# Four late weight loads in unequal pieces: shifting rows between the two halves of the DMA engines

## The chip, the cores and the metric

The kernel runs on one core of one Trainium2 chip. The metric is the device time of one execution in microseconds, the median of several. The core has five engines with queues of their own: TensorE (PE, matrix products; its weight loads are a second row, PEld), VectorE (DVE), ScalarE (ACT), GpSimd (POOL) and SyncE (SP). Data comes from memory through 16 DMA engines. GpSimd issues most of the transfers here (queue q0); instructions, too, are fetched through these engines (q8).

## The reference

Two stages. A sparse attention over 8 batches of 576 positions with 8 heads of 64: half of the heads see a local window of 32, the others every 32nd position. Its output is x, 576 x 512 per batch. Then a spectral mix:

```python
X = np.fft.rfft(x, axis=1)
Xr, Xi = (np.real(X[:, :n_modes]), np.imag(X[:, :n_modes]))          # 64 modes
Yr = np.einsum('bmd,mde->bme', Xr, w_r) - np.einsum('bmd,mde->bme', Xi, w_i)
Yi = np.einsum('bmd,mde->bme', Xr, w_i) + np.einsum('bmd,mde->bme', Xi, w_r)
Y[:, :n_modes] = Yr + 1j * Yi
y = np.fft.irfft(Y, n=S, axis=1)
u = x + y
return (u + np.maximum(u @ w_ch, 0.0)).astype(np.float32)
```

Every mode has its own 512 x 512 matrices w_r and w_i in 4-byte floats, 134 MB for all 64. They are read once, and each is used for only 8 batches.

## The kernel before

The weights are taken in two halves of 256 input rows (all 64 modes of the one half, then all of the other). A tile holds a pair of modes: partitions 0 to 63 hold the real parts, 64 to 127 the imaginary ones. The transfer converts to 2-byte floats on its way.

```python
NWBUF = 5
GUEST = {1: "Y0", 2: "X0", 7: "YT"}      # three early pairs in tiles that are free then

def w_fetch(n=1):
    for _ in range(n):
        i = len(w_tiles)
        if i >= 2 * NM:
            return
        half, m = 1 - i // NM, i % NM
        if i // 2 in GUEST:
            wt = big.tile([128, 2, 4, DM], F16, tag=GUEST[i // 2], name="wt")
        else:
            wt = pw.tile([128, 2, 4, DM], F16, tag="w", name="wt")
        for ri, src in enumerate((moe_w_r, moe_w_i)):
            dst = wt[ds(64 * ri, 64)]
            rows = src[m : m + 2, ds(256 * half, 256), :].rearrange(
                "m (p c) e -> p m (c e)", c=4
            )
            dst = dst.rearrange("p m c e -> p m (c e)")
            ones = range(2)
            if ri and not m:
                ones = [1]
            elif i < 2 * NM - 4:
                nc.gpsimd.dma_start(dst, rows)        # 64 rows x 2 modes x 2048
                continue
            for j in ones:
                nc.gpsimd.dma_start(dst[:, j], rows[:, j])
        w_tiles.extend((wt[:, 0], wt[:, 1]))
```

Pairs are counted from 0 to 63; the last two are loaded one mode at a time. A mode is 16 products of 128x128 weights with 16 columns, and at the end of a pair the next tile is asked for:

```python
def mode(slot, m):
    ...
    for e in range(4):
        for c in range(4):
            nc.tensor.matmul(
                yv[:, mi, e, :], wt[pr, XC[c], ds(128 * e, 128)],
                Xh[half][pr, c, :, :, m], start=(c == 0), stop=(c == 3),
            )
    if m % 2 and (slot or m // 2 not in GUEST):
        w_fetch()
```

The strided heads' inputs are 72 rows for a batch and tensor, loaded as 64 and 8 rows. There are twelve such 8-row transfers, all early, in the order v, q, k for batches 0, 2, 4 and 6:

```python
def load_str(b, nb):
    for vi in (2, 0, 1):
        ...
        if nb == 2:
            nc.gpsimd.dma_start(two[0:64], src[0:64])
        else:
            nc.gpsimd.dma_start(ring[0:64, n, :], src[0:64, b % 2])
        if b % 2 == 0:
            nc.gpsimd.dma_start(two[64:72], src[64:72])
```

The second slot of modes ends so (`again` is n products whose result nobody reads, to keep TensorE going):

```python
for m in range(END, NM):            # modes 54 to 63
    mode(1, m)
    if m < END + 2:
        ...
    else:
        again(0 if m < NM - 6 else 4 if m < NM - 2 else 2)
spec_last(0)
...                                 # inverse transforms, relu, sums, output: all after mode 63
```

The mask `cMl` (128 x 256) is read by the attention over local windows only, which is over when the second slot begins.

Of the kernel before, what the change touches and what calls it, by code (L numbers as in the profile page):

```python
# [79 lines left out]
def kernel(  # L80
# [10 lines left out]
    nc = tc.nc  # L91
# [16 lines left out]
    def psum(kind, half=False):  # L108
# [8 lines left out]
        for n, h in zip(names, hosts)  # L117
# [3 lines left out]
    cs = {  # L121
        n: consts.tile(
            [128, h.shape[1] + more.get(n, 0), *h.shape[2:]], F16, name=n + "_s"
        )
        for n, h in zip(names, hosts)
    }
# [40 lines left out]


    GUEST = {1: "Y0", 2: "X0", 7: "YT"}
    w_tiles = []  # L170
    w_chs = {}
    w_ch = big.tile([128, 4, DM], F16, name="w_ch")

    def w_fetch(n=1):
        for _ in range(n):
# [16 lines that stand above are left out]
                ones = range(2)  # L192
                if ri and not m:
                    ones = [1]
                elif i < 2 * NM - 4:
                    nc.gpsimd.dma_start(dst, rows)  # L196
                    continue
                for j in ones:
                    nc.gpsimd.dma_start(dst[:, j], rows[:, j])
            w_tiles.extend((wt[:, 0], wt[:, 1]))  # L200
# [335 lines left out]
    def mode(slot, m):  # L536
# [8 lines left out]
        for e in range(4):  # L545
            for c in range(4):
# [6 lines left out]
                )  # L553
        if m % 2 and (slot or m // 2 not in GUEST):
            w_fetch()
# [146 lines left out]
    const_load(nc.sync, "cMl", "cFl", "cA")  # L702
    load_str(2, 2)
    w_fetch()

    def str_front(b):
# [39 lines left out]
    for b in range(B):  # L746
        if b in (1, 3):
            load_str(b + 3, 2)
        load_loc(*[(), (), (), (), (0,), (1, 2), (3,), (4, 5)][b])
        w_fetch([2, 1, 1, 1, 1, 1, 0, 0][b])  # L750
        front = str_front(b + 1) if b + 1 < B else loc_front(0)
        for t in range(6):
            str_scores(b, t)
            if b > 0:
                if t < 2:
                    str_values(b - 1, 4 + t)
                elif t == 2:
                    dft(b - 1, 1)
            if t >= 2:
                str_values(b, t - 2)  # L760
            for w in front[SPLIT[t] : SPLIT[t + 1]]:
                w()
        if b == 1:
            nc.vector.memset(PL[:, 0:PS0], 0.0)
# [10 lines left out]
    for b in range(B):  # L775
# [12 lines left out]
        n = 0  # L788
        nm = NMODES[b]
        for mi in range(nm):  # L790
# [3 lines left out]
            n = upto  # L794
# [46 lines left out]
    n = 0  # L841
# [4 lines left out]
    for m in range(END):  # L846
# [7 lines left out]
        n = upto  # L854
# [165 lines left out]
```

The softmax here doesn't subtract the row's maximum and nothing guards it: scores larger than these inputs give would overflow.

## Time and profile before

| what | value |
|---|---|
| time, median of 3 | 434.31 us (433.63 to 435.55) |
| span of the profiled execution | 434.2 us |
| TensorE busy | 338.5 us (78%) |
| VectorE, ScalarE, GpSimd busy | 215.9, 187.5, 129.3 us |
| moved by DMA | 92.18 MB written on the chip's side, 212 GB/s in the mean |
| weight transfers of 512 KB | 62 real, 60 imaginary; 19.0 and 19.4 us from issue to landing |
| weight transfers of 256 KB (one mode) | 4 real, 6 imaginary |

The profile's page cuts the span into 40 equal slices and gives each engine's busy share in tenths; a digit of 9 is 90% or more. Its chain is followed back from the last instruction, at each step to what released it. A line of a group or of the timeline reads: line, engine, operation, output<-inputs, sizes, count, and what ended the idle time before it. "DMA share" is the mean busy share of the 16 DMA engines; it can come out slightly above 1, since packets of one engine overlap a little.

### The profile page before, as it was taken

The numbers are of one execution on the slowest core, as the hardware profiler recorded it, in microseconds if no ns is written. First come the engines' busy times: TensorE is split into PE (matmuls) and PEld (weight loads), VectorE is DVE, ScalarE is ACT, GpSimd is POOL, SyncE is SP. The second block draws the span as 40 slices with busy tenths as digits, with TensorE's granted clock in tenths as the row PEclk, the third lists the DMA queues.
The fourth block names the chain that finished last, engine by engine and source line by source line (L and its number), as shares of the span: only waits on it lengthen the run. The fifth ranks groups of instructions, "written<-read, shape, count | busy, mean of one in ns | idle before, by whom it ended". The sixth has DMA issues, their size and how long they took to land.

```text
span 434.2 us, 12103 instructions
## 1 busy us (share of the span) xinstructions
PE 338.5 (78%) x5307; PEld 244.5 (56%) x5307; DVE 215.9 (50%) x468; ACT 187.5 (43%) x352; POOL 129.3 (30%) x208
## 2 busy tenths in 40 slices
PE   1986888779985787889885566587789798968993
PEld 1865776658864575667753344454456465643441
DVE  2888678744433243342511033355436366503894
ACT  1686678634643435444440401143215123602892
POOL 6433332322332222222222222222222221200992
PEclk9999899865985859875865569887958899988999
DMA  8999999999999999999999999999999999991787
GB/s 176 210 211 213 214 212 213 211 211 213 213 212 212 214 214 212 214 214 213 214 212 213 213 214 214 212 214 215 211 214 214 212 214 214 213 182 30 272 330 261
DMA packets 29140, 92.18 MB, mean 212 GB/s; under 512 B 4064, under 2 KB 5344, under 8 KB 29088
## 3 DMA queue, kind: packets, MB, share of 16 engines
q0 software_dynamic: 24704, 81.28, 94.4%
q1 hardware_dynamic: 3584, 9.59, 5.9%
q8 instruction: 42, 0.69, 0.6%
q10 hardware_dynamic: 800, 0.54, 0.5%
q14 instruction: 10, 0.08, 0.0%
HBM read 163.22 MB, written 9.44 MB: 398 GB/s over the span
## 4 chain that ended last, share of the span: by engine, by line
DMA 68%; PE 19%; DVE 6%; ACT 2%; issue 2%; POOL 1%; DVEq 0%; POOLq 0%
DMA wt<-in_moe_w_i_dram 51%; DMA wt<-in_moe_w_r_dram 11%; DMA ring<-in_q_dram 5%; PE y L547 2%; PE v L689 2%; DVE xb L250 2%; DVE kz L292 2%; PE u L689 2%; PE v L895 2%; PE sc L514 1%; ACT X L260 1%; PE tp L395 1%; DVE rec L249 1%; PE sc L441 1%; PE sc L353 1%
## 5 line engine op out<-in xcount | busy, mean ns | idle before, releaser
L547 PE MATMUL y<-X,wt 128*128 128x16 f16 (+1 forms) x2048 | 82.4, 192 | 61.0 <-DMA wt<-in_moe_w_i_dram 59.4
L547 PEld LDWEIGHTS <-wt 128*128 128x128 f16 (+1 forms) x2048 | 72.9, 103 | 76.5 <-issue 68.5
L196 POOL DMA_DIRECT2D wt<-in_moe_w_r_dram x62 | 36.5, 589 | 141.7 <-PE y L547 67.4
L196 POOL DMA_DIRECT2D wt<-in_moe_w_i_dram x60 | 35.4, 590 | 73.5 <-DMA wt<-in_moe_w_i_dram 61.2
L654 ACT ACTIVATE v<-sc 128x512 f16<-128x512 f32 x32 | 19.1, 597 | 69.7 <-PE sc L645 69.6
L645 PE MATMUL sc<-w_cp,xT 128*128 128x512 f16 (+1 forms) x160 | 48.2, 430 | 0.0
L471 ACT ACTIVATE PL<-sc 128x480 f16<-128x480 f32 (+1 forms) x48 | 27.3, 580 | 46.8 <-PE sc L457 46.5
L655 DVE COPY xo<-tp 128x512 f16<-128x512 f16 x32 | 22.1, 692 | 35.7 <-PE tp L653 35.6
L249 DVE RECIPROCAL rec<-av 90x4 f32<-90x4 f32 (+2 forms) x80 | 14.7, 184 | 46.2 <-PE av L486 34.8
L250 DVE TENSOR_TENSOR xb<-av,rec 90x256 f16<-90x256 f32 (+2 forms) x80 | 36.0, 450 | 2.7
L402 DVE COPY qT<-tp 128x576 f16<-128x576 f16 x16 | 12.0, 758 | 38.8 <-PE tp L395 35.9
L260 ACT ACTIVATE v<-tp 128x640 f16<-128x640 f16 (+1 forms) x24 | 19.4, 808 | 24.9 <-PE tp L429 22.1
L395 PE MATMUL tp<-cI_s,ring 64*64 64x64 f16 x864 | 26.7, 213 | 0.8 <-DVE qT L402 0.6
L360 ACT ACTIVATE PL<-sc 90x360 f16<-90x360 f32 (+1 forms) x48 | 22.7, 491 | 6.1 <-PE sc L353 5.3
L929 DVE TENSOR_TENSOR osb<-u,rl 128x512 f32<-128x512 f32 (+1 forms) x37 | 23.7, 674 | 1.8 <-PE u L689 1.1
L395 PEld LDWEIGHTS <-ring 64*64 64x64 f16 x864 | 21.1, 125 | 5.7 <-issue 2.6
L910 POOL TENSOR_TENSOR rl<-rl,xo 128x512 f32<-128x512 f32 x16 | 18.3, 1157 | 18.2 <-ACT rl L908 17.9
L441 PE MATMUL sc<-cMl_s,cI_s 128*128 128x480 f16 (+1 forms) x48 | 22.5, 468 | 1.6 <-ACT X L260 1.6
L457 PE MATMUL sc<-qT,kz 128*128 128x160 f16 (+1 forms) x160 | 22.4, 267 | 0.0
L908 ACT ACTIVATE rl<-v 128x512 f32<-128x512 f32 x36 | 20.4, 600 | 4.7 <-PE v L689 3.9
L285 PE MATMUL tp<-cI_s,ring 72*128 72x72 f16 x256 | 15.1, 206 | 9.4 <-DMA ring<-in_v_dram 7.9
L260 ACT ACTIVATE kz<-tp 64x360 f16<-64x360 f16 (+1 forms) x32 | 19.1, 595 | 7.7 <-PE tp L395 6.1
(103 smaller groups left out, 655.7 us busy)
## 6 DMA issues: line engine op xcount, KB each, us to landing
wt<-in_moe_w_r_dram POOLq DMA_DIRECT2D x62, 512.0 KB, 19.0
wt<-in_moe_w_i_dram POOLq DMA_DIRECT2D x60, 512.0 KB, 19.4
out_dram<-osb SPq DMA_DIRECT2D x14, 512.0 KB, 2.7
ring<-in_v_dram POOLq DMA_DIRECT2D x8, 288.0 KB, 13.3
ring<-in_q_dram POOLq DMA_DIRECT2D x8, 288.0 KB, 13.6
ring<-in_k_dram POOLq DMA_DIRECT2D x8, 288.0 KB, 13.5
ring<-in_v_dram POOLq DMA_DIRECT2D x3, 512.0 KB, 15.0
ring<-in_q_dram POOLq DMA_DIRECT2D x3, 512.0 KB, 14.8
```

The lines of the kernel that those rows point to most:

```text
L196: nc.gpsimd.dma_start(dst, rows)
L250: nc.vector.tensor_tensor(out=dst, in0=val.rearrange("p h (q c) -> p h c q", c=4), in1=rec[0:n, 0:pieces] .to_broadcast((n, pieces, 64)) . ...
L260: nc.scalar.activation(out=out, in_=in_, func=ACTF.Copy)
L360: nc.scalar.activation(out=PS[0:n, ds(POFF[t], 4 * n)], in_=scp[0:n, 0 : 4 * n], func=ACTF.Exp, scale=SCALE,)
L395: nc.tensor.transpose(tp[ds(64 * hp, 64), ds(64 * i, 64)], qn[ds(64 * hp, 64), ds(64 * (9 * g + i), 64)], idn[ds(64 * hp, 64), ds(64 * hp, ...
L441: nc.tensor.matmul(scp[:, 0 : n * times].rearrange("p (h x) -> p h x", h=times), idn, mask_rows("cMl", n, times), start=True, stop=False,)
L457: nc.tensor.matmul(scp[:, ds(col, n)], kzs[par][:, hp, ds(s0, 128)], qTs[par][:, ds(s0, n)], start=False, stop=(i == len(todo) - 1),)
L471: nc.scalar.activation(out=dst, in_=src, func=ACTF.Exp, scale=SCALE)
L547: nc.tensor.matmul(yv[:, mi, e, :], wt[pr, XC[c], ds(128 * e, 128)], Xh[half][pr, c, :, :, m], start=(c == 0), stop=(c == 3),)
L645: nc.tensor.matmul(vp[pr, :], xT[:, ch, cols], w_chs["cp"][:, ch, :], start=(ch == 0), stop=(ch == 3),)
L655: nc.vector.tensor_copy(out=xo[pr].rearrange("p (h q c) -> p h q c", h=2, c=4), in_=tp[pr, 0:512].rearrange("p (h c q) -> p h q c", h=2, c=4),
L929: nc.vector.tensor_tensor(out=osb[:, t % 2, cols], in0=up[:, cols], in1=rls[b, t][:, t % 2, cols], op=AluOp.add,)
```

## The change

The real part of four late pairs (36, 41, 46 and 51) is loaded as 48, 8 and 8 rows in place of 64. Between the two 8-row pieces stands an 8-row transfer of next to nothing (8 rows of 2 x 8 elements of `w_ch` into the mask tile, which is free by then); its data is never read. A second one follows the real part of the next pair. Each of the eight writes to a place of its own, so none waits for another's write. They are there to turn the choice of DMA engines: an 8-row transfer occupies eight of the 16, and the next one the others, so with a turn in between both 8-row pieces go to the same eight. The purpose is to give those eight more of the weights and the other eight less. The bytes of the weights stay the same, and so does all arithmetic.

```diff
+    UNEVEN = (36, 41, 46, 51)
...
+    turns = []
+
+    def turn_engines():
+        n = len(turns)
+        turns.append(n)
+        dst = cs["cMl"][0:8, ds(32 * n, 32)].rearrange("p (a x) -> p a x", a=2)
+        src = moe_w_ch[0:8].rearrange("p (a x) -> p a x", a=2)
+        nc.gpsimd.dma_start(dst[:, :, 0:8], src[:, :, 0:8])
...
                 if ri and not m:
                     ones = [1]
+                elif i // 2 in UNEVEN and not ri:
+                    nc.gpsimd.dma_start(dst[0:48], rows[0:48])
+                    nc.gpsimd.dma_start(dst[48:56], rows[48:56])
+                    turn_engines()
+                    nc.gpsimd.dma_start(dst[56:64], rows[56:64])
+                    continue
                 elif i < 2 * NM - 4:
                     nc.gpsimd.dma_start(dst, rows)
+                    if not ri and i // 2 - 1 in UNEVEN:
+                        turn_engines()
                     continue
```

## The prediction

> **What bounds the kernel now.** I read four views, from the whole to the end. First the page's 40 slices, its DMA queues and its chain:
>
> ```profile
> PE   1986888779985787889885566587789798968993
> DMA  8999999999999999999999999999999999991787
> q0 software_dynamic: 24704, 81.28, 94.4%
> q8 instruction: 42, 0.69, 0.6%
> q14 instruction: 10, 0.08, 0.0%
> DMA 68%; PE 19%; DVE 6%; ACT 2%; issue 2%; POOL 1%; DVEq 0%; POOLq 0%
> ```
>
> The DMA row stands at 9 from the second slice to the 36th: the weights' queue (q0) keeps all 16 engines full up to some 390 us, and then a tail of 41 us follows in which they no longer matter. 68% of the chain is DMA. Then the waits of TensorE in the second half, and the busy time in stretches around the last weights:
>
> ```profile
> PE y L547 <- DMA wt<-in_moe_w_i_dram: 41.0, 23, 4.2
> ```
>
> ```profile
> core 0: us, PE busy (x) PEld busy (x) DVE busy (x) ACT busy (x) POOL busy (x), PEclk, DMA share, GB/s
> 378.00:387.50 9.50, 6.01 (x91) 3.83 (x92) 0.71 (x2) 0.18 (x1) 1.55 (x3) 0.84 1.05 210
> 388.00:392.00 4.00, 2.94 (x42) 1.61 (x40) 0.56 (x1) 0.00 (x0) 0.00 (x0) 1.00 0.54 108
> 392.00:393.00 1.00, 0.12 (x5) 0.15 (x5) 0.00 (x0) 0.00 (x0) 0.00 (x0) 1.00 0.31 61
> 393.00:394.00 1.00, 0.96 (x18) 0.46 (x16) 0.00 (x0) 0.00 (x0) 0.00 (x0) 1.00 0.02 4
> ```
>
> This is the view that the change is about. From 388 to 392 the share of DMA is 0.54: half of the engines are done some 5 us before the other half, and every transfer is finished only when its slowest engine is. The end itself, on TensorE (start, duration, what it waited for):
>
> ```profile
> 384.17 0.64 PE L547 MATMUL y<-X,wt 128*128 128x16 f16 x16 [3.26 <-DMA wt<-in_moe_w_i_dram]
> ...
> 392.88 0.64 PE L547 MATMUL y<-X,wt 128*128 128x16 f16 x16 [1.95 <-DMA wt<-in_moe_w_i_dram]
> ...
> 394.08 0.64 PE L547 MATMUL y<-X,wt 128*128 128x16 f16 x16
> ```
>
> Modes 62 and 63 start at 392.88 and 394.08 because their weights land then; what follows hangs on mode 63. So the time moves one to one with the last landing.
>
> **Which engines are late, and why.** The packet records behind the DMA row have no engine numbers, but they can be linked: in the full stretch a 4 KB packet takes 324 ns, the next on its engine starts 305 ns after it, and a 64-row transfer gives each engine 8 packets and a completion write, 2457.6 ns in all, over and over. An instruction fetch (q8: 16 KB, 892 to 975 ns) breaks exactly one such rhythm and sets it back by 0.9 to 1.16 us, some 1.1 in most. The fetches take turns over 8 engines: their durations repeat with a period of 8, and an engine hit by one fetch is hit again 8 fetches later. 40 fetches fall before the last weight, five on each of the eight: about 5 us, which is the gap above. The last packets of the eight end at 392.4, 392.6 (four of them), 393.1, 393.2 and 393.6 us.
>
> **What the skill says.** "DMA: Bandwidth & Descriptors", section "Why a DMA increments its semaphore by 16 and not by 1": a transfer uses the largest number of engines up to 16 that divides its slowest dimension; from the software queue, fewer than 16 are consecutive engines from a round-robin cursor. The trace agrees: in the 8-row loads of the strided heads eight engines move two packets each and eight move none, and the next 8-row load takes the other eight. The same section says that only the full count of all 16 means landed, which is the 0.54 stretch seen from the waiting side. Its section "Issuing engines are not separate DMA queues" says that all queues run on the same 16 engines; the fetches of q8 delaying q0 show it. I find no page that says which engines fetch instructions.
>
> **The change, part by part.**
> 1. Real part of an uneven pair: 48 rows are 3 rows, 6 packets, on each engine. The first 8-row piece puts 2 packets on eight engines, the turning transfer moves the cursor on by eight, the second piece meets the same eight again. So a half H has 10 packets and the other half L has 6, where all had 8. The second turning transfer, before the imaginary part of the next pair, puts the cursor back, so all four pairs load the same H. Sum: 4 x 2 x 0.305 us = 2.44 us more on H, 2.44 us less on L.
> 2. Extra transfers: 3 in each uneven pair and 1 in the next, 16 in all. In the 8-row loads an engine with data pays one more completion write (20 ns), one without pays some 15 ns over the usual (its writes follow at 3, 19 and 6 ns). Four pairs: 4 x (2 x 20 + 2 x 15) = 0.3 us on H; about as much on L, as the turning transfers' tiny packets run there. An estimate from these rows: +0.3 us on both.
> 3. GpSimd's issues: 16 more by 0.57 us (the 8-row loads' median) = 9 us spread over 100 us of the engine's idle time; not on the path.
> 4. Buffers and depth: a transfer issues only when the one eight before it has landed (eight completion semaphores in turn). Landing takes 19.4 us, eight times 2.46, so the line is full now. Around an uneven pair the eight places hold small pieces: at least 22 packets, 6.7 us, stay queued on the slowest engine. It doesn't run dry.
> 5. TensorE, VectorE and ScalarE: the same instructions; only landing times shift.
>
> So everything hangs on whether H keeps clear of the eight fetching engines. If L were exactly these, they would end 2.44 - 0.3 = 2.1 us earlier (393.6 -> 391.5), the others at about 391, and the time would be 434.3 - 2.1 = 432.2 us.
>
> **Is it so? What the trace says.** I followed the 16 rhythms through the loads of batches 4 and 6 (the 7th to 12th 8-row transfer). The pieces that the change adds are transfers 13, 15, 17, ...: odd in that count, the half that carried the first (v) 8-row piece of batch 4. Call it H. The third and fourth fetch of the steady part (the two of 893 ns) hit engines of H: one whose completion was due at 57.12 us (raw time) vanished from its place and came 877 ns later, and it is hit again by the fetch eight places on. The next six (949, 945, 935, 974, 974, 961 ns) hit engines of L. So the fetching eight are 6 in L and 2 in H; the halves that the cursor makes stand two engines off. Then:
> - six fetching engines in L end about 2.1 us earlier, the last at 391.5;
> - two fetching engines in H end later. Followed to the end they are among the early ones of the eight, at 392.4 and 392.6; with 2.44 + 0.3 they end at 395.2 and 395.3 us;
> - six others in H, done near 387.5 to 388, end near 390.5.
> The last landing moves from 393.6 to about 395.3, by +1.7 us; mode 62 from 392.88 to 394.6, mode 63 from 394.08 to 395.8. Time: 434.3 + 1.7 = 436.0 us.
>
> **Rivals.**
> - *The halves fit in the changed run* (432.2 us). The size of the change speaks for it: four pairs shift 4.9 us between the halves, the very gap, as if made for halves that fit. If the cursor's place at the start is left over from what ran before, it can differ from this trace. Against it: the one trace I have says 6 and 2, and both kernels move the cursor by whole turns (12 x 8 = 96, and 16 more x 8), so neither shifts it for the next.
> - *The line runs shallow*: with eight places full of small pieces the engines could starve. 6.7 us are left on the slowest; engines of L that don't fetch may idle, but they are up to 10 us ahead and end nothing. Worth 0, or +0.5 us if issue latency bites.
> - *It is hidden anyway*: if the tail were held by ScalarE or VectorE, 434.3 would stay. Against it stand the wait of 1.95 us before mode 62 and the full TensorE after mode 63.
> - *Completion overhead is larger than thought*, because small packets cost more than their bytes: 16 transfers at 0.1 us would add 1.6 us to either case.
>
> **Range and chances.** I give the halves as in the trace 70%, fitting halves 25%, no effect 5%. Two peaks, 432.2 and 436.0, each with some 0.6 us of spread between runs (433.63 to 435.55 before): 432.0 to 437.2 holds a little over eight in ten. I name 435.8, a little under the upper peak. All of this is below 1%: faster by over 2% 0.01, within 2% 0.975, slower by over 2% 0.015.
>
> **What would show it.** In the changed kernel's stretches after 388 us, a half-filled DMA (0.5) that is gone, with the last weights landing near 391.5, shows the fitting halves. A step that thins out early and a thin rest (two engines of 16, a share near 0.13) up to 395 shows the 6 and 2. Mode 63 at about 392 or about 395.8 decides. The 8-row pieces must give two packets to eight engines and both pieces to the same ones; if the heavy half changes from pair to pair, step 1 is wrong and the time stays. A wait of GpSimd on small pieces with DMA below 9 in slices 22 to 32 would show the shallow line. The prediction is wrong if the time falls below 432 or if the last landing moves and the end doesn't.

## The result and the profile after

| kernel | median | lowest to highest | runs |
|---|---|---|---|
| before | 434.53 us | 433.63 to 435.85 | 6 |
| changed | 438.0 us | 436.74 to 439.75 | 6 |

The ratio is 1.0077, with a 95% interval of 1.0056 to 1.0099: the change makes the kernel 3.5 us slower. The prediction was 435.8 us, with 437.2 as its upper end. The time is some 2 us longer than the profiled span in all these runs.

The page of the changed kernel, the rows that were shown for the kernel before, and the GB/s row:

```profile
DMA  8999999999999999999999999999999999990787
GB/s 172 204 210 213 214 212 213 212 210 212 213 213 213 213 213 214 213 214 213 215 212 213 214 204 213 212 211 213 210 213 191 206 212 215 212 210 18 276 330 262
DMA 74%; PE 14%; DVE 5%; issue 3%; ACT 2%; POOL 1%; DVEq 0%; POOLq 0%
```

The DMA row still stands at 9 through the weights, and DMA's share of the chain went from 68% to 74%. But slices 24 and 31 moved 204 and 191 GB/s where their neighbours moved 213: the engines were busy there, and slower. Next the busy time in stretches (length; busy time of the five engines; TensorE's clock; DMA share; GB/s):

```profile
core 0: us, PE busy (x) PEld busy (x) DVE busy (x) ACT busy (x) POOL busy (x), PEclk, DMA share, GB/s
388.00:392.00 4.00, 4.00 (x52) 2.05 (x49) 0.00 (x0) 0.00 (x0) 0.35 (x1) 0.61 1.07 215
392.00:393.00 1.00, 1.00 (x7) 0.43 (x6) 0.00 (x0) 0.00 (x0) 0.00 (x0) 0.84 0.54 102
393.00:394.00 1.00, 1.00 (x20) 0.69 (x19) 0.34 (x1) 0.00 (x0) 0.00 (x0) 1.00 0.33 66
394.00:396.00 2.00, 0.42 (x2) 0.00 (x0) 0.22 (x1) 0.00 (x0) 0.00 (x0) 1.00 0.12 25
```

The half-filled stretch from 388 to 392 (0.54 before) is full now, and at the end a share of 0.12 is left, which is two engines of 16. TensorE's timeline at the end:

```profile
396.25 0.64 PE L565 MATMUL y<-X,wt 128*128 128x16 f16 x16 [1.83 <-DMA wt<-in_moe_w_i_dram]
...
397.51 0.64 PE L565 MATMUL y<-X,wt 128*128 128x16 f16 x16 [0.18 <-DMA wt<-in_moe_w_i_dram]
```

Modes 62 and 63 start at 396.25 and 397.51 us, 3.4 us later than before; the last weights land at 397.0 instead of 393.6. The span grew by 1.8 us only (436.0 against 434.2), because the part from mode 63 on took 38.5 us here and 40.1 in the profiled run of before, with TensorE's clock in the six microseconds after mode 63 at 1.00 and 0.72. The change is not the reason: of the sixteen runs below, ten have 38.0 to 38.8 us there at a clock of 1.00, and three have 40.2 to 40.4 at 0.72 or 0.73. So a single execution can be some 2 us longer or shorter for this alone, and I go by the landings in a trace and by the medians of the times.

There is one more thing to take off. Count the 4 KB packets of the weights' queue in the order of their starts, and ask how much later the same number starts than in the trace of before; I call it the **lag**. It shows how far the engines together are behind. It is 0.5 us at 70 us already, where the two kernels do the same, and still 0.5 ahead of the first uneven pair. So of the 3.4 us between the two landings 2.9 can be the change's; the medians differ by 3.5 us (2.4 to 4.3).

**Where the other half came from.** Compare the stretch around the last uneven pair. Before:

```profile
core 0: us, PE busy (x) PEld busy (x) DVE busy (x) ACT busy (x) POOL busy (x), PEclk, DMA share, GB/s
330.00:335.00 5.00, 4.97 (x77) 3.44 (x75) 3.38 (x8) 4.32 (x8) 1.84 (x4) 1.00 1.06 212
335.00:340.00 5.00, 3.34 (x71) 2.68 (x69) 3.42 (x7) 2.17 (x4) 1.48 (x3) 1.00 1.06 215
```

and changed:

```profile
330.00:335.00 5.00, 4.80 (x66) 3.06 (x65) 3.22 (x8) 3.02 (x6) 0.58 (x1) 0.91 1.06 184
335.00:340.00 5.00, 3.81 (x62) 2.57 (x59) 2.93 (x8) 3.23 (x6) 2.92 (x5) 1.00 1.01 181
```

The DMA share hardly moves (1.06, 1.01), but GB/s falls to 184 and 181: 10 us x (213 - 182.5) / 213 = 1.4 us lost on the mean engine. The packet records say how: 114 packets of 4 KB took 345 to 1006 ns instead of 324, together 18.5 us of engine time too long, and 3.3 us more of idle engines; (18.5 + 3.3) / 16 = 1.4 us again. In the trace of before no 10 us between 60 us and the last weights lose more than 0.6 us of engine time in this way. I call it a slow stretch. The lag says the same: 0.5 us ahead of pair 36, 1.4 at 325 us and 3.0 at 350. The last uneven pair costs the mean engine 1.6 us, the three before it 0.9 together. How much of it fell on the two engines of the thin rest is an estimate: linked back from the last two landings, 1.65 and 1.1 us between 334 and 346 us, but inside a slow stretch more than one link fits.

TensorE's modes are a poorer measure. Against the kernel before they are 1.5 us late at mode 100 and 3.9 at mode 104, a step of 2.4 us; but the ninth run below, which has no uneven pair at that place, steps from -0.3 to 1.3 between the same two modes.

What GpSimd, which issues the loads, did there (start, duration, idle time before and what ended it):

```profile
318.81 0.56 POOL L182 DMA_DIRECT2D cMl_s<-in_moe_w_ch_dram  x1 [1.90 <-DMA wt<-in_moe_w_r_dram]
321.27 0.55 POOL L209 DMA_DIRECT2D wt<-in_moe_w_r_dram  x1 [1.90 <-DMA wt<-in_moe_w_i_dram]
...
329.42 0.57 POOL L182 DMA_DIRECT2D cMl_s<-in_moe_w_ch_dram  x1 [2.38 <-DMA wt<-in_moe_w_r_dram]
333.04 0.58 POOL L212 DMA_DIRECT2D wt<-in_moe_w_i_dram  x1 [3.06 <-DMA wt<-in_moe_w_i_dram]
```

Each small piece waits for the landing of a whole earlier transfer, 2.46 us at the steady pace, as if it were 512 KB itself. While it holds its place among the eight, that much less data is queued. So the theory that the experiments test has two terms: **misfit** (two fetching engines stand in the heavy half, +1.7 us, as predicted) and **the short line** (small pieces use up places, the engines that are ahead run short, and a slow stretch follows that hits the late engines too). The prediction had allowed 0 to 0.5 us for the second.

### The profile page after: what moved, and what is told of

Its sections match the earlier page's. It is cut to its first block, busy times and chain, and to the rows that moved or that the text cites. A ratio compares the mean times of both kernels' runs of the same rounds, so it can differ in the third digit from the quotient of the medians.

```text
span 436.0 us, 12125 instructions
## 1 busy us (share of the span) xinstructions
PE 335.1 (77%) x5307; PEld 241.8 (55%) x5307; DVE 215.6 (49%) x468; ACT 187.4 (43%) x352; POOL 137.5 (32%) x224
## 4 chain that ended last, share of the span: by engine, by line
DMA 74%; PE 14%; DVE 5%; issue 3%; ACT 2%; POOL 1%; DVEq 0%; POOLq 0%
DMA wt<-in_moe_w_i_dram 45%; DMA wt<-in_moe_w_r_dram 19%; DMA ring<-in_k_dram 6%; DMA ring<-in_q_dram 3%; PE v L707 2%; PE u L707 2%; PE v L913 2%; PE sc L532 1%; DVE kz L310 1%; DVE xb L268 1%; DMA ring<-in_v_dram 1%; PE y L565 1%; ACT X L278 1%; POOL wt L212 1%; PE av L392 1%
## 5 line engine op out<-in xcount | busy, mean ns | idle before, releaser
L212 POOL DMA_DIRECT2D wt<-in_moe_w_r_dram x58 | 34.0, 586 | 113.4 <-PE y L565 45.2
L672 ACT ACTIVATE v<-sc 128x512 f16<-128x512 f32 x32 | 19.1, 597 | 73.3 <-PE sc L663 73.2
L663 PE MATMUL sc<-w_cp,xT 128*128 128x512 f16 (+1 forms) x160 | 49.5, 439 | 0.0
```

Of the source, the lines that this page charges most:

```text
L663: nc.tensor.matmul(vp[pr, :], xT[:, ch, cols], w_chs["cp"][:, ch, :], start=(ch == 0), stop=(ch == 3),)
```

## The experiments

Times are medians; each ratio is against runs of the kernel before on the same chip. "Lost" is engine time per 10 us in packets over 324 ns.

**1 to 3. Shift the halves.** If another start of the cursor makes the light half fit the fetching engines, the change pays. A tiny transfer of r rows moves the cursor by r; it is put back after pair 52.

```diff
+                    if i // 2 == 36:
+                        move_cursor(2)          # second run: (8, 4, 2); third: (8)
...
+                        if i // 2 == 52:
+                            move_cursor(8, 4, 2)  # second run: (2); third: (8)
```

> One 2-row transfer before the first uneven pair moves the cursor by 2 (8, 4 and 2 rows after the last one bring it back). Misfit theory: the heavy half then meets either none or four of the eight fetching engines. None: no half-filled and no thin stretch before the last weights, which land near 391.5; time 432.2 us if the pieces themselves cost nothing, 434 us if they cost 1.7 us in any case (line theory). Four: a thin rest of four engines (DMA share near 0.25) before the end, time 437 to 438.5 us. Line theory alone (the halves do not matter): 438 us, as in the changed kernel.

> The same with 14 before (8, 4 and 2 rows) and 2 after. Misfit theory: the other of the two outcomes of the +2 run, that is four heavy fetching engines and 437 to 438.5 us if +2 met none, and 432.2 to 434 us if +2 met four. Line theory alone: 438 us.

> One 8-row transfer before and one after: the other half is the heavy one, and six fetching engines are in it. Misfit theory: a thin rest of six engines (share near 0.37) before the last weights; the last landing was 393.6 and moves by 2.44 + 0.3, time 437.2 us, or 438.9 us with 1.7 us for the pieces. Line theory alone: 438 us.

Measured: +2 gives 438.14 us (ratio 1.0074, 1.0052 to 1.0096), -2 gives 440.45 (1.0116, 1.0082 to 1.0149), +8 gives 439.85 (1.0106, 1.0067 to 1.0145), all against 435.09. None fits. The +2 run looks like the four heavy engines of the misfit theory (a DMA share of 0.27 from 394 to 396 us); then -2 should have fitted, and it took longer than any time expected for it. The +8 run, too, is above all that was expected. With +8 the roles are exchanged: the rest is thick, eight to six engines from 395 to 396 us, where it was two:

```profile
core 0: us, PE busy (x) PEld busy (x) DVE busy (x) ACT busy (x) POOL busy (x), PEclk, DMA share, GB/s
393.00:394.00 1.00, 1.00 (x14) 0.62 (x13) 0.00 (x0) 0.00 (x0) 0.00 (x0) 0.95 1.06 209
394.00:396.00 2.00, 1.21 (x16) 0.48 (x12) 0.56 (x1) 0.00 (x0) 0.00 (x0) 1.00 0.62 123
```

That is the misfit seen from the other side, though not alone: the +8 run also lost 22.5 us in slow packets at 300 to 320 us. The -2 run is spoilt as a test of fit: its three extra transfers in a row at pair 36 left 4 active engines of 16 at one moment near 256 us and 33 us of idle engine time, and the +2 run has 28 us of it at 330 to 340 us: the first signs that the line itself matters.

**4. The same pieces, balanced.** The turn stands behind both 8-row pieces, so they go to opposite halves: all small transfers remain, but no half gets more.

```diff
                     nc.gpsimd.dma_start(dst[48:56], rows[48:56])
-                    turn_engines()
                     nc.gpsimd.dma_start(dst[56:64], rows[56:64])
+                    turn_engines()
```

> The turning transfer stands after the two 8-row pieces, so they go to different halves and each engine has 8 packets as before; the same number and sizes of transfers. Misfit theory: the half-filled stretch of 5 us stays, the last weights land where they did, time 434.5 to 434.9 us. Line theory (the small pieces cost 1.7 us or more by themselves): 436.2 us or more.

Measured: 436.05 us against 435.09, ratio 1.0022 (1.0010 to 1.0034). That is +1.0 us (0.4 to 1.5), between the two expectations, which were 0.4 us at most and 1.7 us at least. So the pieces by themselves cost about 1 us, and most of the 3.5 us comes from the unevenness or through it. In stretches:

```profile
core 0: us, PE busy (x) PEld busy (x) DVE busy (x) ACT busy (x) POOL busy (x), PEclk, DMA share, GB/s
392.00:393.00 1.00, 0.00 (x0) 0.00 (x0) 0.00 (x0) 0.00 (x0) 0.00 (x0) 1.00 0.52 102
393.00:394.00 1.00, 0.57 (x17) 0.60 (x18) 0.00 (x0) 0.00 (x0) 0.00 (x0) 1.00 0.31 61
394.00:396.00 2.00, 1.78 (x25) 0.75 (x22) 0.29 (x1) 0.00 (x0) 0.00 (x0) 0.99 0.00 0
```

The half-filled end is back (0.52) and there is no thin rest: the last weights land at 394.2 us. Lost at 330 to 340 us: 2.4 us, not 18.5. (Near the first of the four pairs, at 255 to 265 us, it lost 6 us.)

**5 to 7. Shifts spread over earlier pairs, and uneven pairs further apart.** The shift by 14 again, its small transfers now at pairs 20, 24 and 28 (fifth run) or 8, 9 and 10 (sixth); the sixth and seventh have their uneven pairs at 13, 25, 39 and 53, the seventh without a shift.

```diff
+    MOVES = {20: 8, 24: 4, 28: 2, 54: 2}    # sixth run: {8: 8, 9: 4, 10: 2, 58: 2}
...
-    UNEVEN = (36, 41, 46, 51)
+    UNEVEN = (13, 25, 39, 53)               # sixth and seventh run
```

> The cursor is moved by 14 as in the -2 run, but by three tiny transfers far apart (after the real parts of pairs 20, 24 and 28) and back by 2 after pair 54, so that the first uneven pair meets a full line; the rest as in the changed kernel. If the -2 run lost its time only because its three moving transfers emptied the line at pair 36, and its halves do fit: no half-filled and no thin stretch at the end, last weights near 391.5 to 392.5, time 2 us below before, 433 us. If small pieces in late pairs cost time whatever the halves: 437 to 440 us, as in the three shifted runs so far.

> Fitting halves (14 moved after pairs 8, 9 and 10), and the four uneven pairs spread over the run (13, 25, 39, 53), one after each round of eight fetches, so that no engine gets more than some 2 us ahead. Theory of the runaway engines (engines far ahead run dry while small pieces hold the eight places, and come back together with long packets): no burst of long packets anywhere, time 2 us below before, 433 us, the last weights at 391.5. If the pieces cost time by themselves: 435 us or more.

> The changed kernel's halves (two fetching engines in the heavy half) with the uneven pairs at 13, 25, 39 and 53. Misfit alone: a thin rest of two engines (share 0.13), mode 63 later by 1.7 us, time 436.6 us. If the remaining 1.3 us of the changed kernel come from engines running ahead they stay away here unless the last pair meets a lead of over 7 us; if the lead does it again at pair 53: 438 us.

Measured: 438.36 (ratio 1.0082, 1.0057 to 1.0107), 437.47 (1.0059, 1.0037 to 1.0081) and 438.10 us (1.0084, 1.0055 to 1.0112), all against 434.81. My halves were wrong again: two engines stay in a thin rest in all three, to 395.7, 396.9 and 397.4 us. And setting the pairs apart did not remove the slow stretches (13.0 us lost at 340 to 350 us in the seventh run).

**8 and 11. Drain the line alone.** The kernel before with seven, then four, tiny 16-row transfers ahead of pair 36. Each gives every engine a packet or two of 16 bytes, so nothing becomes uneven; only places are taken.

```diff
+                    if i // 2 == 36 and not ri:
+                        for _ in range(7):      # eleventh run: 4
+                            move_cursor(16)
```

> The kernel before, with seven 16-row transfers of next to nothing ahead of pair 36: no engine gets more than another, but seven of the eight places hold nothing. Theory of the empty line: the number of active engines falls well below 16 near 256 us, packets of 0.5 to 1 us follow, and the time rises by 1.5 to 2.5 us, to some 437 us, with all engines late alike and the 5 us stretch of eight engines at the end shorter or gone. If a drained line costs nothing because the queue is refilled in time: 435 us.

> The kernel before with four tiny 16-row transfers ahead of pair 36, where the run with seven of them took 5.2 us more. Theory: about four of the eight places in the line can be spared, so the engines hardly run dry: +0.3 to +1.0 us, 435.1 to 435.8, and few packets over 345 ns near 256 us. Rival, each place taken costs the same: four sevenths of 5.2 us, +3.0 us, 437.8.

Measured: seven give 440.0 us against 434.81 (1.0112, 1.0085 to 1.0140), +5.2 us and more than expected; four give 435.29 against 435.06 (1.0007, 0.9994 to 1.0020), within the measurement. GpSimd with seven, and the stretches:

```profile
251.33 0.50 POOL L182 DMA_DIRECT2D scrap<-in_moe_w_ch_dram  x1 [1.94 <-DMA wt<-in_moe_w_i_dram]
253.75 0.50 POOL L182 DMA_DIRECT2D scrap<-in_moe_w_ch_dram  x1 [1.92 <-DMA wt<-in_moe_w_r_dram]
256.54 0.58 POOL L209 DMA_DIRECT2D wt<-in_moe_w_r_dram  x1 [2.30 <-DMA wt<-in_moe_w_i_dram]
257.12 0.60 POOL L209 DMA_DIRECT2D wt<-in_moe_w_i_dram  x1
```

```profile
core 0: us, PE busy (x) PEld busy (x) DVE busy (x) ACT busy (x) POOL busy (x), PEclk, DMA share, GB/s
252.00:256.00 4.00, 2.05 (x31) 1.46 (x28) 2.31 (x6) 0.00 (x0) 0.50 (x1) 0.50 0.42 74
256.00:260.00 4.00, 3.70 (x46) 2.41 (x46) 1.04 (x2) 0.60 (x1) 3.46 (x7) 0.50 0.59 84
```

From the third on, every tiny transfer waited for one full landing (1.9 to 2.0 us), while nothing replaced what landed; then all was empty (shares 0.42 and 0.59, 77 us of idle engine time) and eight loads went out one behind the other without a wait. With four, the same place keeps its share:

```profile
252.00:256.00 4.00, 1.98 (x39) 1.57 (x39) 1.85 (x6) 0.00 (x0) 1.12 (x2) 0.50 1.11 201
256.00:260.00 4.00, 3.08 (x30) 1.86 (x28) 1.85 (x4) 0.60 (x1) 2.96 (x6) 0.50 1.02 190
```

It does have a slow stretch (201 and 190 GB/s, 13.8 us lost) and yet costs nothing measurable: the lag grows by 1.0 us there and stays, but the last weights land only 0.2 us later than before. So a slow stretch is not always time. I read this as engines that end early having lost what they could spare; which engines lost it was not followed.

**9 and 10. Take the change apart.** Three uneven pairs without the last; then the last alone.

```diff
-    UNEVEN = (36, 41, 46, 51)
+    UNEVEN = (36, 41, 46)                   # tenth run: (51,)
```

> The changed kernel with three uneven pairs (36, 41, 46) in place of four. Theory A, the emptied line: with less lead for the eight light engines they do not run dry at the last uneven pair, so there is no stretch of lengthened packets near 330 us and no jump of 2.4 us in the modes' lateness there; modes 100 to 120 about 1.5 us late as before it, last landing about +1.5 to +1.9 us over the kernel before, time about 436.0 to 436.5. Rival B, every uneven pair costs the same share: three quarters of the changed kernel's 3.5 us, time 437.2, modes late in equal steps. Theory C, misfit alone: two heavy engines fetch instructions and carry 3 x 0.61 us more plus overhead, +1.3 us, 435.9.

> Only the last of the four uneven pairs (51), everything else as before. Theory A, the line empties at the fourth uneven pair because the light engines are far ahead by then: alone it is as harmless as the first was, modes up to 0.8 us late after it, last landing at most +0.8 us, time 434.9 to 435.6. Rival, the place itself is costly (pair 51 meets the fetches of the last bands): the step of 2.4 us stays, time about 437.2.

Measured: three give 436.32 (1.0032, 1.0018 to 1.0046), the last alone 435.39 (1.0009, 0.9997 to 1.0022), both against 435.06. That is +1.3 and +0.3, and 1.6 us is not 3.5: by the times, **the parts don't add up**. In the trace with three pairs no slow stretch stands out (at most 3.4 us lost in any 10 us), and the thin rest is there and ends sooner:

```profile
core 0: us, PE busy (x) PEld busy (x) DVE busy (x) ACT busy (x) POOL busy (x), PEclk, DMA share, GB/s
392.00:393.00 1.00, 0.43 (x3) 0.00 (x0) 0.23 (x1) 0.00 (x0) 0.00 (x0) 1.00 0.12 25
393.00:394.00 1.00, 0.41 (x14) 0.44 (x15) 0.00 (x0) 0.00 (x0) 0.00 (x0) 1.00 0.14 29
```

So this trace shows the misfit nearly by itself. Its last weights land at 394.4 us, 0.7 later than before, and its lag ahead of pair 36 is -0.1, so 0.8 us are added. The prediction's terms give 392.6 + 3 x 0.61 + 0.2 = 394.6 us, +1.0 and not three quarters of 1.7, because the two heavy engines first use up the 1.0 us by which they were ahead of the last one. But the profiled execution was the fastest of the twenty (435.13 us; the median is 436.32), so the other executions may well have slow stretches. The tenth run is a half miss: I expected no slow stretch with one uneven pair, and it has one of the largest (27 us of engine time lost at 320 to 340 us, down to 178 GB/s):

```profile
325.00:330.00 5.00, 3.70 (x30) 2.27 (x31) 0.99 (x2) 0.59 (x1) 0.99 (x2) 0.72 1.12 178
330.00:335.00 5.00, 4.97 (x74) 3.39 (x73) 3.69 (x9) 3.34 (x6) 1.75 (x4) 0.94 1.02 187
```

By the median of the times it costs 0.3 us. This trace doesn't show it as free: the last weights land at 395.31 us, 1.7 later than before, of which 0.6 was there before pair 51 (the lag) and 1.0 came after it. The part after mode 63 was short here, 38.0 us against 40.1. Taken by landings, three pairs add 0.8 us, the last alone 1.0 and all four together 2.9: the parts don't add up here either, but 1.0 us is missing and not 1.9.

**12. Mark the cursor.** The kernel before with a 2-row tiny transfer at every second pair from 44 to 58.

```diff
+                    if 44 <= i // 2 < 60 and i % 4 == 0 and not ri:
+                        move_cursor(2)
```

> The kernel before with a two-row tiny transfer after the real part of every second pair from 44 to 58, eight in all, which together take the cursor round once and mark two engines each as early or late. If six or eight engines fetch instructions in the order worked out from the earlier runs (0 or 1, 6 or 7, 9 to 14), the marks in the order 0-1, 2-3, ... 14-15 show late engines in the first, the fourth (or third), the fifth and then two late ones in the sixth and seventh and one in the eighth. Time: single places taken with whole transfers between them, so no emptied line: +0 to +0.6 us; but from one mark to the next the real parts start 2 engines on, and with 64 rows they stay even, so no shift: 434.8 to 435.4. A rival that each tiny transfer costs 0.5 us would give 438.8.

Measured: 435.55 against 435.06 (1.0012, 0.9998 to 1.0026). The two packets of each mark ran at (us):

```
291.79 293.11 | 302.42 303.45 | 311.48 315.74 | 321.62 325.61 | 331.03 336.16 | 345.86 345.92 | 355.81 357.14 | 361.18 366.89
```

Four marks have an early and a late engine (4 to 5.7 us apart), the first two only early ones and the sixth and seventh only late ones (they continue the row of the late packets, some 10 us from mark to mark). That is 4 + 4 = 8 late engines in this trace, but not in the order that I had written down: counted from the first mark, one each of 4-5, 6-7, 8-9 and 14-15, and all of 10 to 13. A window of eight from 0 holds two of them, the complement six, as in the changed kernel; and no window of eight neighbours avoids all, since one late engine stands at 14 or 15 and another at 4 or 5. That fits the shifts, none of which helped.

**13 to 16. The missing term.** The parts left 1.9 us by the times, 1.0 by the landings. First, a shortened line at pair 51 without a fourth uneven pair: the ninth kernel with four tiny transfers ahead of pair 51.

```diff
-    UNEVEN = (36, 41, 46, 51)
+    UNEVEN = (36, 41, 46)
...
+                    if i // 2 == 51 and not ri:
+                        for _ in range(4):
+                            move_cursor(16)
```

> Three uneven pairs (36, 41, 46) and four tiny 16-row transfers ahead of pair 51, which take places in the line without making a pair uneven. Theory: the line empties at pair 51, the early engines come back in step, and the packets of the two engines that are already last lengthen by 1 to 1.7 us: 436.3 + 1.1 to 1.7 = 437.4 to 438.0. Rival, the emptied line costs nothing (as four such transfers ahead of pair 36 did in the kernel before, +0.2): 436.3 to 436.6.

Measured: 437.83 us against 434.63 (1.0072, 1.0046 to 1.0097), inside the theory's range and outside the rival's. Four tiny transfers cost 0.2 us in the kernel before and some 1.7 us here (1.0072 less 1.0032, of 434.6; with the two intervals some 0.5 to 3 us), where two engines are already last. Its trace has two slow stretches:

```profile
305.00:310.00 5.00, 4.21 (x52) 2.64 (x50) 1.94 (x5) 1.19 (x2) 1.36 (x3) 0.86 1.08 190
330.00:335.00 5.00, 3.44 (x52) 2.57 (x51) 2.63 (x6) 2.95 (x5) 2.17 (x4) 0.87 1.03 200
```

The second is the one that was meant; the lag grows by 1.1 us over it, from 2.4 to 3.5. The first stands at pair 46, ahead of the added transfers, where the program is still that of the ninth run, whose trace has 208 GB/s there. So the same program has a slow stretch in one execution and none in another. That a slow stretch is dearer where two engines are already last fits these runs but is not shown: the two drains stand at different pairs (36 and 51), and four tiny transfers ahead of pair 51 in the kernel before were not run.

Then the other half, four uneven pairs without the slow stretch. I moved them forward.

```diff
-    UNEVEN = (36, 41, 46, 51)
+    UNEVEN = (31, 36, 41, 46)               # last run: (10, 14, 18, 22)
...
+    scrap = big.tile([128, 32 * 16], F16, name="scrap")   # not in the first of the three
-        dst = cs["cMl"][0:8, ds(32 * n, 32)].rearrange("p (a x) -> p a x", a=2)
+        dst = scrap[0:8, ds(32 * n, 32)].rearrange("p (a x) -> p a x", a=2)
```

> Four uneven pairs at 31, 36, 41 and 46, none at 51. Theory, misfit and the lengthened packets at pair 51 are two terms: only the misfit is left, which the prediction put at 1.7 us, so 436.5 to 437.0 us, the modes' lateness without the jump of 2.4 us at 330 us, two engines in the thin rest to about 395.3. Rival, the fourth uneven pair costs most wherever it stands: 438 us as the changed kernel.

> Four uneven pairs at 31, 36, 41 and 46, none at 51, the turning transfers written to a place that nothing else uses. Theory, misfit and the lengthened packets at pair 51 are two terms: only the misfit is left, which the prediction put at 1.7 us, so 436.3 to 437.0 us, the modes' lateness without the jump of 2.4 us at 330 us, two engines in the thin rest to about 395.3. Rival, the fourth uneven pair costs most wherever it stands: 438 us as the changed kernel.

> Four uneven pairs at 10, 14, 18 and 22, the turning transfers written to a place of their own. Theory, the line empties only where the fast engines are far ahead, and the misfit is a term of its own: no lengthened stretch (under 3 us of engine time in any 10 us), two engines in the thin rest at the end, +1.7 us over the kernel before (1.2 to 2.2). Rival, an uneven pair empties the line wherever it stands: lengthened stretches in the early part too, and +3 us or more.

The first of the three took 448.93 us and says nothing on the question: at pair 31 the turning transfers go into the mask that the attention over local windows still reads (they change it), and GpSimd then stood 13.27 us waiting for TensorE's modes. With a place of their own: 437.62 against 435.92 (1.0045, 1.0028 to 1.0062), +1.7 us in number as expected (the time itself is above the range, because the kernel before took 435.92 us on that chip), but the trace has a slow stretch at pair 46 (19.1 us lost at 300 to 310 us), so it isn't the misfit alone. The last was to settle that and turned out against me: 438.73 against 434.71 (1.0094, 1.0064 to 1.0124), +4.0 us, with 20.7 us lost at 160 to 200 us. A place early in the program does not protect. The four-pair misfit was never had without a slow stretch; with three pairs it was, in one trace.

## Why the prediction was wrong, step by step

- **Which engines are late: right.** The 16-byte packets of the changed kernel's first turn, which run on the light half, came at 251.61 and 252.44 us, then six from 254.99 to 256.79: two early engines and six late ones, so two late ones are in the heavy half. The thin rest of 0.12 is these two.
- **Step 1, 2.44 us: right; step 2, 0.3 us: too small for all that the pieces do.** In the ninth run a heavy engine can be followed through pair 46: six packets, then two and two, end at 302.07, 302.70 and 303.34 us, started at 300.22; 3.12 us where the usual is 2.46. That is 0.66 us for 0.61 plus overhead, and the second turn adds 0.03. But with the pieces balanced, where step 2 is all that is left, the fourth run took 1.0 us more (0.4 to 1.5).
- **Step 3, GpSimd's issues off the path: right.** They took 0.56 us each (0.57 predicted). What I did not count is that each waits for a landing.
- **Step 4, "It doesn't run dry", and the rival's "Worth 0, or +0.5 us if issue latency bites": this failed.** The 22 packets were worked out for the slowest engine alone, and I took that for enough. Engines ran short (some 13 of 16 active at the least near 334 us), and packets lengthened: the mean engine lost 1.6 us at the last uneven pair. What the prediction's +1.7 us leaves unexplained, and what this term of 0 to 0.5 us has to hold, is 1.2 us by the landings (2.9 less 1.7) and 1.8 us by the times (3.5 less 1.7). The fourteenth run, which shortens the line after three uneven pairs, gives some 1.7 us, with the wide interval and the doubts named there.
- **Step 5, the last landing: right in its logic, wrong in its size.** It was to move by +1.7 us and is 3.4 us later in the trace, 393.6 to 397.0, with 0.5 of it from before the kernels differ. Mode 63 followed it (397.51 instead of 395.8). The median time did, too (438.0 instead of 436.0), but a single execution need not: the part after mode 63 alone varies by 2 us.
- **The sign that I had named for the short line was blind.** "DMA below 9 in slices 22 to 32": the digits stay at 9, because a packet that takes 1000 ns is as busy as one of 324. GB/s showed it (191 in slice 31).
- **Fitting halves (25%)**: by the marks of the twelfth run no start of the cursor gives them.

What stays open: why packets lengthen (it mostly goes with engines that run short, but in the fifteenth run 19 us were lost at 300 to 310 us with no idle engine there), why the same pieces make a slow stretch in one execution and not in another (pair 46 in the fourteenth run and in the ninth), and whether pair 51 is a costly place by itself. A further way, small pieces that meet only fetch-free positions of the cursor, would need still more transfers in the line; it wasn't tried.

## What to carry to other kernels

Before cutting a load into pieces, count places in its queue as well as bytes: a piece of next to nothing holds its place until it has landed (13.0 us in the median for the turning transfers, 19 us for a full one), and a line that is a few places short was free in one kernel here and cost some 1.7 us in another. Look for lost bandwidth in GB/s, not in the busy share, and ask which engine lost it: a loss on an engine that ends early need not be time. Costs measured one at a time need not add up, so try the disturbances together as well. And before a trace is taken for the kernel, see where its execution stands among the times: the fastest of twenty can lack just what the median has.

## What the runs showed of the hardware

- A line that is really emptied ahead of pair 36 (seven of eight places taken by tiny transfers) costs 5.2 us, more than twice what I had expected; four places cost 0.2 us.
- 4 KB packets of 324 ns stretched to 0.35 to 1.0 us in the changed kernel (2.5 us at most, in the run with three uneven pairs and four tiny transfers) after small transfers had taken places in the line.
- The eight engines that the instruction fetches set back are not neighbours in the order in which small transfers take engines: two positions only early, two only late, four mixed among the eight marks.
